# Sketched attention and a top-2 router of experts on one core: expert blocks in waves, a rebuilt attention, resident second layers

## The chip, the cores and the metric

The kernel runs on one core of a Trainium2 chip. The metric is the device time of one execution in microseconds. Every core has five engines with an instruction queue each: PE (TensorE, matrix products), DVE (VectorE), ACT (ScalarE), POOL (GpSimd) and SP (SyncE, which here only issues transfers). The engines meet by semaphores. In the profile PE's weight loads are a row of their own, PEld.

## The reference

Four batches of four heads, 1088 positions, head size 32, all in float32. Each row of q and k is projected by two 8 x 32 sketches, and the outer product of the two results gives 64 features; attention is linear in them. Its output `x` (4352 tokens of 128) goes to a router that adds scaled noise to eight logits and takes the two best of eight experts. An expert is two layers of 128 to 1024 to 128 with a relu between.

```python
phi(x) = outer(S1 x, S2 x)                       # 64 features
kv = phi(k).T @ v ;  z = phi(k).sum(seq)
x = (phi(q) @ kv) / (phi(q) @ z + 1e-6)          # heads side by side: 4352 x 128
noisy = x @ w_gate + log1p(exp(x @ w_noise)) * noise
out = sum over the top 2 experts e of  weight_e * relu(x @ w1[e]) @ w2[e]
```

## The kernel before

It has three stages, one after another.

*Attention and router*, for one batch after the other (`attention`). `key_values` transposes the keys on PE (L288), sketches them (L255), builds 64 features per head in one DVE product (L249) and sums `phk.T @ [v, 1]` over eight 128-row tiles and a rest (L304, L306). `queries` takes four tiles of queries at a time: transposes (L331), two 512-column products with both sketches (L336, L337), their product on DVE (L341), the product with `kv` (L350), and the division by the denominators (L356 to L358). `router` transposes `x` again (L369), multiplies it by the gate and noise weights (L374), runs some thirty small DVE instructions with Exp and Ln on ACT between them (L391 to L427), counts how many tokens of earlier rows go to each expert by two products with triangles and ones (L435, L436), and sends each token's two gated copies to its experts' regions of `xs` in HBM: eight indirect scatters of POOL per four tiles (L453).

*Table.* After the last token, `table` turns the counts into blocks of rows, each with an expert and a first row, read later into registers of SP (`number`, L549).

*Experts.* `blocks` walks 23 blocks of 256 rows and 21 of 128 rows mixed, then the four 256-row blocks of the fullest expert. For each, SP loads the rows (L568) and both layers of the expert, 512 KB each (L560, L561); PE transposes the rows (L596), makes the hidden layer in chunks of 512 columns (L673, here 256 columns wide for a large block), ACT or DVE applies the relu in turn (L588, L590), and the second layer follows two chunks later (L632). POOL scatters the result to `parts` (L657). Before the last expert's rows are added, `combine` sums the two parts of every token into the output; the fullest expert's rows are then added to the output by eight accumulating scatters (L648).

The order on each engine is made when the program is built, by a scheduler that takes the ready instruction of the highest priority (the earlier in the program text), with its own estimates of durations. On the chip every engine keeps to that order: PE waits at an instruction even if later ones are ready. Float32 products are shown in the trace as two records each, with a weight load each, transposes as one.

Of the kernel before, what the change touches and what calls it, by code (L numbers as in the profile page):

```python
# [8 lines left out]
F32 = mybir.dt.float32  # L9
# [12 lines left out]
def kernel(  # L22
# [14 lines left out]
    nc = tc.nc  # L37
    P = nc.NUM_PARTITIONS
# [5 lines left out]
    FJ = F // P  # L44

# [6 lines left out]
    A1 = DH + 1  # L52
# [5 lines left out]

    N = B * S
    PAIRS = 2 * N  # L60
    NL = PAIRS // E // (2 * P)
    NB = -(-(PAIRS - 2 * P * NL - E * (2 * P - 1)) // (2 * P))
    NS = (PAIRS - 2 * P * (NL + NB) + E * (P - 1)) // P
    CAP = N + P
    XW = D + 1
    I32 = mybir.dt.int32
# [4 lines left out]
    small = ctx.enter_context(tc.tile_pool(name="small", bufs=3))  # L71
    moe = ctx.enter_context(tc.tile_pool(name="moe", bufs=3))
    hpool = ctx.enter_context(tc.tile_pool(name="hpool", bufs=4))
    wpool = ctx.enter_context(tc.tile_pool(name="wpool", bufs=5))
    xpool = ctx.enter_context(tc.tile_pool(name="xpool", bufs=8))
    ypool = ctx.enter_context(tc.tile_pool(name="ypool", bufs=8))
    cpool = ctx.enter_context(tc.tile_pool(name="cpool", bufs=2))
    dram = ctx.enter_context(tc.tile_pool(name="dram", bufs=1, space=DRAM))
    ps_a = ctx.enter_context(tc.tile_pool(name="ps_a", bufs=3, space=PSUM))
    ps_h = ctx.enter_context(tc.tile_pool(name="ps_h", bufs=3, space=PSUM))  # L80
# [5 lines left out]

    words = const.tile([P, 2 * R, 2], U32, name="words")
    for i, s in enumerate((S1, S2)):
        src = s.bitcast(U32).rearrange("r (d w) -> d r w", w=2)
        for c in range(4):  # L90
            nc.scalar.dma_start(words[DH * c:DH * (c + 1), R * i:R * (i + 1), :], src)

    def u32(name):
        return const.tile([P, 2 * R], U32, name=name)

    lo_w, hi_w = words[:, :, 0], words[:, :, 1]
    expo, head, b1, b2, b3 = (u32(n) for n in ("expo", "head", "b1", "b2", "b3"))

    def bits(o, x, s1, op0, s2=None, op1=None):
        if op1 is None:  # L100
            nc.vector.tensor_scalar(out=o, in0=x, scalar1=s1, scalar2=None, op0=op0)
        else:
            nc.vector.tensor_scalar(out=o, in0=x, scalar1=s1, scalar2=s2, op0=op0, op1=op1)

    bits(expo[:], hi_w, 20, ALU.logical_shift_right, 0x7FF, ALU.bitwise_and)
    bits(expo[:], expo[:], 896, ALU.max, 896, ALU.subtract)
    bits(expo[:], expo[:], 23, ALU.logical_shift_left)
    bits(head[:], hi_w, 0x80000000, ALU.bitwise_and)
# [4 lines left out]
    for b_ in (b1, b2, b3):  # L113
        nc.vector.tensor_tensor(out=b_[:], in0=b_[:], in1=head[:], op=ALU.bitwise_or)
# [38 lines left out]
    for e in range(E):  # L153
        nc.gpsimd.memset(rank[:, e:e + 1], float(E - e))
# [599 lines left out]
```

## Time and profile before

| | |
|---|---|
| runs | 637.64, 638.33, 638.45 us (median 638.33) |
| profiled execution | 637.79 us, of which 636.1 us are the span of the trace |
| busy: PE / PEld | 469.1 us (74%) / 408.6 us (64%) |
| busy: DVE / ACT / POOL | 198.5 / 119.3 / 174.7 us |
| matrix products and transposes recorded | 2781 |
| mean granted clock of TensorE | 0.799 of full speed |
| moved by DMA | 80.27 MB, 126 GB/s |

Shares of the whole span say little here: the stages have different limits, and the rows further down give each stage apart. "Idle before" of an engine is time in which it stood before the named kind of instruction, and the releaser is what ended that wait. The ends of matrix products are modelled, so the distance between two starts says more about PE's pace than a duration.

### The profile page before, as it was taken

The numbers are of one execution on the slowest core, as the hardware profiler recorded it, in microseconds if no ns is written. First come the engines' busy times: TensorE is split into PE (matmuls) and PEld (weight loads), VectorE is DVE, ScalarE is ACT, GpSimd is POOL, SyncE is SP. The second block draws the span as 40 slices with busy tenths as digits, with TensorE's granted clock in tenths as the row PEclk, the third lists the DMA queues.
The fourth block names the chain that finished last, engine by engine and source line by source line (L and its number), as shares of the span: only waits on it lengthen the run. The fifth ranks groups of instructions, "written<-read, shape, count | busy, mean of one in ns | idle before, by whom it ended". The sixth has DMA issues, their size and how long they took to land.

```text
span 636.1 us, 8071 instructions
## 1 busy us (share of the span) xinstructions
PE 469.1 (74%) x2781; PEld 408.6 (64%) x2781; DVE 198.5 (31%) x687; ACT 119.3 (19%) x232; POOL 174.7 (27%) x236
## 2 busy tenths in 40 slices
PE   0278547847575757854518999999999999999950
PEld 0275337534563456423307999999999999999950
DVE  3112444152513451155371222222232222223430
ACT  0101330121203120132201222222212122221100
POOL 3300155106330524023420313232222313132016
PEclk9999575566557755656557999999999999999995
DMA  8841010001000100000129977868686867750753
GB/s 213 277 164 35 4 63 30 4 1 34 14 19 1 34 4 30 0 14 21 34 57 323 304 235 207 258 197 257 193 255 205 245 222 236 236 150 9 246 189 29
DMA packets 86296, 80.27 MB, mean 126 GB/s; under 512 B 11875, under 2 KB 76004, under 8 KB 85744
## 3 DMA queue, kind: packets, MB, share of 16 engines
q1 hardware_dynamic: 73152, 65.66, 33.5%
q0 software_dynamic: 5472, 8.96, 4.9%
q10 hardware_dynamic: 7632, 5.15, 2.5%
q8 instruction: 22, 0.36, 0.2%
q14 instruction: 18, 0.15, 0.1%
HBM read 63.44 MB, written 16.75 MB: 126 GB/s over the span
## 4 chain that ended last, share of the span: by engine, by line
issue 36%; PE 28%; DVE 12%; POOL 9%; DMA 6%; ACT 5%; ACTq 2%; POOLq 1%; SPq 0%; DVEq 0%
POOL parts L657 8%; PE bank L336 5%; PE bank L304 5%; PE bank L255 4%; PE bank L337 4%; DMA two<-parts 3%; PE bank L374 3%; PE bank L350 2%; PE bank L331 2%; ACT L395 2%; DVE phk L249 1%; ACT qT L334 1%; POOL out_dram L648 1%; DVE x L358 1%; DVE phq L341 1%
## 5 line engine op out<-in xcount | busy, mean ns | idle before, releaser
L673 PE MATMUL hp<-bT,w 128*128 128x256 f32 (+1 forms) x768 | 157.9, 338 | 2.4 <-DMA w<-in_moe_w_dram 2.0
L632 PE MATMUL acc<-w,h 128*128 128x128 f32 x1200 | 158.2, 275 | 0.5 <-DVE h L588 0.5
L632 PEld LDWEIGHTS acc<-w,h 128*128 128x128 f32 x1200 | 154.2, 192 | 6.2 <-DVE h L588 0.6
L673 PEld LDWEIGHTS hp<-bT,w 128*128 128x128 f32 x768 | 116.5, 194 | 9.2 <-issue 2.4
L657 POOL DMA_INDIRECT parts<-y,xb x67 | 65.8, 983 | 196.6 <-DVE y L588 147.9
L453 POOL DMA_INDIRECT xs<-xg,to x68 | 69.3, 1019 | 160.5 <-issue 59.5
L588 DVE TENSOR_SCALAR h<-hp 128x512 f32<-128x512 f32 x80 | 55.2, 691 | 120.2 <-PE hp L673 120.2
L590 ACT ACTIVATE h<-hp 128x512 f32<-128x512 f32 x70 | 41.8, 597 | 123.9 <-PE hp L673 123.9
L435 PE MATMUL bank<-masks,earlier 128*128 128x32 f32 (+1 forms) x18 | 5.4, 394 | 62.5 <-DVE g L427 62.5
L435 PEld LDWEIGHTS bank<-masks,earlier 128*128 128x128 f32 x18 | 4.5, 312 | 63.2 <-issue 63.2
L255 PE MATMUL bank<-sk,kT 128*128 128x64 f32 x136 | 29.8, 419 | 11.8 <-ACT kT L290 11.3
L304 PE MATMUL bank<-vaug,phk 128*128 128x66 f32 x128 | 29.4, 424 | 12.3 <-DVE phk L249 12.3
L255 PEld LDWEIGHTS bank<-sk,kT 128*128 128x128 f32 x136 | 29.6, 333 | 12.5 <-ACT kT L290 11.7
L336 PE MATMUL bank<-qT,sq 128*128 128x512 f32 (+1 forms) x36 | 29.9, 928 | 9.8 <-ACT qT L334 9.7
L304 PEld LDWEIGHTS bank<-vaug,phk 128*128 128x128 f32 x128 | 27.9, 330 | 13.4 <-issue 9.8
L341 DVE TENSOR_TENSOR phq<-qa,bank 128x512 f32<-128x512 f32 (+1 forms) x18 | 11.8, 658 | 59.1 <-PE bank L337 58.9
L337 PE MATMUL bank<-qT,sq 128*128 128x512 f32 (+1 forms) x36 | 27.4, 857 | 0.0
L596 PE MATMUL bank<-ident,xb 128*128 128x128 f32 x75 | 16.3, 277 | 14.0 <-DMA xb<-xs 14.0
L350 PEld LDWEIGHTS bank<-kv,phq 128*128 128x128 f32 (+1 forms) x144 | 18.2, 201 | 10.3 <-DVE phq L341 4.7
L334 ACT COPY qT<-bank 128x512 f32<-128x512 f32 (+1 forms) x18 | 10.1, 562 | 76.6 <-PE bank L331 76.6
L588 DVE COPY bT<-bank 128x256 f32<-128x256 f32 x21 | 8.9, 425 | 42.7 <-PE bank L596 42.7
L350 PE MATMUL bank<-kv,phq 128*128 128x66 f32 (+1 forms) x144 | 19.0, 285 | 3.4 <-DVE phq L341 3.4
(169 smaller groups left out, 387.5 us busy)
## 6 DMA issues: line engine op xcount, KB each, us to landing
w<-in_moe_w_dram SPq DMA_DIRECT2D x90, 512.0 KB, 4.7
parts<-zeros ACTq DMA_DIRECT2D x4, 1024.0 KB, 8.8
two<-parts SPq DMA_DIRECT2D x6, 640.0 KB, 5.6
xb<-xs SPq DMA_DIRECT2D x27, 129.0 KB, 3.7
kld<-in_k_dram SPq DMA_DIRECT2D x4, 512.0 KB, 4.9
vld<-in_v_dram SPq DMA_DIRECT2D x4, 512.0 KB, 4.0
qld<-in_q_dram SPq DMA_DIRECT2D x4, 512.0 KB, 4.4
out_dram<-one SPq DMA_DIRECT2D x6, 320.0 KB
```

What stands on the lines that cost most here:

```text
L255: nc.tensor.matmul(ps[:, c0:c0 + H * 2 * R], lhsT=kT, rhs=sk[:, i, :], start=(i == 0), stop=(i == 1))
L304: nc.tensor.matmul(o, lhsT=phk[:, t, hs, :].rearrange("p h f -> p (h f)"), rhs=vaug[:, hs, t, :], start=(t == 0), stop=False)
L336: nc.tensor.matmul(pa[:, 0:w], lhsT=sq[:, 0, :], rhs=qT[:, 0:w], start=True, stop=True)
L337: nc.tensor.matmul(pb[:, 0:w], lhsT=sq[:, 1, :], rhs=qT[:, 0:w], start=True, stop=True)
L350: nc.tensor.matmul(ps[rows, c0:c0 + 2 * A1], lhsT=phq[hp][:, P * i + rows.start:P * i + rows.stop], rhs=kv[:, hp, :], start=True, stop=True)
L374: nc.tensor.matmul(ps[:, 2 * E * i:2 * E * (i + 1)], lhsT=xT[:, P * i:P * (i + 1)], rhs=wgn[:], start=True, stop=True)
L453: disjoint("xs", nc.gpsimd.indirect_dma_start(out=xs[:], out_offset=bass.IndirectOffsetOnAxis(ap=to[:, t:t + 1], axis=0), in_=xg[:, t, :], ...
L588: nc.vector.tensor_scalar_max(o, i, 0.0) if relu else nc.vector.tensor_copy(o, i)
L590: nc.scalar.activation(out=o, in_=i, func=AF.Relu) if relu else nc.scalar.copy(o, i)
L632: nc.tensor.matmul(acc[:, D * c:D * (c + 1)], lhsT=h[:, P * (n * i + c):P * (n * i + c + 1)], rhs=w2[:, j, :], start=(j == 0 and c == 0), ...
L657: disjoint("parts", nc.gpsimd.indirect_dma_start(out=parts[:], out_offset=bass.IndirectOffsetOnAxis(ap=to[:, c, :], axis=0), in_=y[:, D * ...
L673: nc.tensor.matmul(hp[:, P * n * i:P * n * (i + 1)], lhsT=w1[:, P * (j0 + i):P * (j0 + i + 1)], rhs=xT[:, 0:P * n], start=True, stop=True)
```

## The change

All three stages are written anew; sizes, inputs, outputs and float32 stay.

- *Waves.* The tokens known after batch 0, 1 and 2 fill at least 9, 18 and 16 blocks of 128 rows whatever the routing is (`full_blocks`; 256 pairs per tile less at most 127 left over per expert). `table` now runs after every batch. Wave 0 (9 blocks) is written beside batch 2's attention, wave 1 (18) beside batch 3's, wave 2 (16) and a last wave of 32 blocks follow. All 75 blocks have 128 rows; before there were 27 of 256 and 21 of 128. A fetch waits only for the scatters of its own batch and earlier ones.
- *Second layers resident.* `load_w2` reads all eight experts' second layers (4 MB) into SBUF once. A block's transfer shrinks to its rows and `w1`. PE reads the block's expert into a register of its own (L601) and computes each of the eight operand addresses by one fused register instruction of four or five operations ("ISA" in the listings, L647).
- *Attention.* Keys and queries share `features`: transposes, a product with both halves of the sketches side by side (128 columns), an add and an outer product on DVE. Query features are then transposed for `attend`. The gate and noise weights are folded into `kv` once per batch, so that `attend` yields numerators, denominators and router scores at once (98 columns); the transposes of `x` and its product with the gate are gone.
- *Router* on 8 or 9 tiles at once instead of four (batch 0 still in two parts); its two count products use a PSUM bank of their own. ACT loads one function table at the start (L184); before, Exp and Ln changed tables 19 times.
- *Start and end.* ACT issues 3 transfers at the start instead of 37; clearing `parts` is gone. Every block scatters to `parts`; `combine` of the first 3200 tokens runs inside the last wave, and the last 1152 tokens are combined at the end in three pieces. The accumulating scatters are gone.

```diff
+    FIRST = [0, NT, 2 * NT + 1, 3 * NT + 1]
+    REST = [2 * NT, 4 * NT + 1]
+    TILES = 4 * NT + 2
+    DONE = [NT, 2 * NT + 1, 3 * NT + 1, TILES]
+    WAVES, used = [], 0
+    for d in DONE[:-1]:
+        WAVES.append(full_blocks(d) - used)
+        used += WAVES[-1]
+    LAST = (PAIRS + E * (P - 1)) // P - used
...
+    w2 = const.tile([P, E * FJ, D], F32, name="w2")
+    def load_w2():
+        for e in range(0, E, 2):
+            nc.sync.dma_start(w2[:, FJ * e:FJ * (e + 2), :],
+                              moe_w2[e:e + 2, :, :].rearrange("o (j p) d -> p (o j) d", p=P))
+    nc.scalar.preload_act_table_set("natural_log_exp_and_others")
...
+    def features(tiles, tag, by_head=False):
+        n = len(tiles)
+        ps = bank()
+        for i, x in enumerate(tiles):
+            nc.tensor.transpose(ps[:, P * i:P * (i + 1)], x, ident[:])
+        xT = work.tile([P, 512], F32, name="xT", tag="xT", bufs=3)
+        nc.scalar.copy(xT[:, 0:P * n], ps[:, 0:P * n])
+        ps = bank()
+        for i in range(n):
+            nc.tensor.matmul(ps[:, P * i:P * (i + 1)], lhsT=xT[:, P * i:P * (i + 1)],
+                             rhs=sk[:].rearrange("p i h r -> p (i h r)"), start=True, stop=True)
+        two = ps[:, 0:P * n].rearrange("p (a i b y) -> p a i b y", a=n, i=2, b=H)
+        ab = work.tile([P, G, H, 2, R], F32, name="ab", tag="ab", bufs=3)
+        o = ab[:, 0:n].rearrange("p a b w r -> p b a (w r)" if by_head else "p a b w r -> p a b (w r)")
+        nc.scalar.copy(o, two[:, :, 1])
+        V.tensor_tensor(out=o, in0=two[:, :, 0], in1=o, op=ALU.add)
+        phi = work.tile([P, G, H, RR], F32, name=tag, tag="phi", bufs=5)
+        th = ab[:, 0:n].rearrange("p t h w r -> p (t h) w r")
+        V.tensor_tensor(
+            out=phi[:, 0:n].rearrange("p t h (i j) -> p (t h) i j", i=R),
+            in0=th[:, :, 0, :].unsqueeze(3).to_broadcast([P, H * n, R, R]),
+            in1=th[:, :, 1, :].unsqueeze(2).to_broadcast([P, H * n, R, R]), op=ALU.mult)
+        return phi
...
+                    lhsT = two_heads(phis[t // G], t % G, hp)
+                    rhs = vld[:, hp, :, t, :]
+                else:
+                    lhsT = rp[r0:r0 + HALF, 2 * hp:2 * hp + 2, :].rearrange("p h f -> p (h f)")
+                    rhs = v_rest[r0:r0 + HALF, b // 2, hp, :, :]
+                nc.tensor.matmul(ps[:, W * hp:W * (hp + 1)], lhsT=lhsT, rhs=rhs, start=(t == 0 and hp == 0),
+                                 stop=(t == NT), skip_group_check=True)
+        kv = kvs[b]
+        both = ps[:, 0:2 * W].rearrange("p (a x) -> p a x", a=2)
+        upper, lower = slice(0, 2 * RR // 2), slice(RR, 2 * RR)
+        V.tensor_copy(kv[upper, :, 0:DH + 1], both[upper, :, 0:DH + 1])
...
+        ps = bank()
+        for hp in range(2):
+            nc.tensor.matmul(ps[:, 2 * E * hp:2 * E * (hp + 1)], lhsT=kvT[:, P * hp:P * (hp + 1)], rhs=wgn[:, hp, :],
+                             start=(hp == 0), stop=True, skip_group_check=True)
+        both = ps[:, 0:4 * E].rearrange("p (a x) -> p a x", a=2)
+        V.tensor_copy(kv[upper, :, KC:KC + 2 * E], both[upper, :, :])
+        nc.scalar.copy(kv[lower, :, KC + 2 * E:YC], both[lower, :, :])
...
+        phT = []
+        for hp in range(2):
+            ps = bank()
+            for i in range(n):
+                nc.tensor.transpose(ps[:, P * i:P * (i + 1)], two_heads(phi, i, hp), ident[:])
+            t = work.tile([P, 512], F32, name="phT", tag="phT", bufs=4)
+            nc.scalar.copy(t[:, 0:P * n], ps[:, 0:P * n])
...
+            ps = bank()
+            for i in range(i0, i0 + m):
+                for rows, kv in kvs_of[i]:
+                    for hp in range(2):
+                        c0 = 2 * YC * (i - i0) + YC * hp
+                        nc.tensor.matmul(
+                            ps[rows, c0:c0 + YC], lhsT=phT[hp][:, P * i + rows.start:P * i + rows.stop],
+                            rhs=kv[:, hp, :], start=True, stop=True)
+            nc.scalar.copy(nd[:, at + i0:at + i0 + m].rearrange("p t a y -> p (t a y)"), ps[:, 0:2 * YC * m])
...
-            e = number(tab, 2 * k, E - 1)
-            r = number(tab, 2 * k + 1, E * CAP)
-            return [(rows(r, n), *weights(e), n, False)]
...
+    def evict(o, i, relu=False, spread=True):
+        if spread and turn[0] % 2:
+            V.tensor_scalar_max(o, i, 0.0) if relu else V.tensor_copy(o, i)
+        else:
+            nc.scalar.activation(out=o, in_=i, func=AF.Relu) if relu else nc.scalar.copy(o, i)
+        turn[0] += 1
+    def wave(tab, step, K, spread, old=0):
...
+        def fetch(i):
+            e = value(tab, 0, i, E - 1)
+            r = value(tab, 1, i, E * CAP)
+            xb = xpool.tile([P, XW], F32, name="xb", tag="xb")
+            load_ = nc.sync.dma_start(xb[:], xs[bass.ds(r, P), :])
+            behind("xs", load_, step)
+            w1 = wpool.tile([P, F], F32, name="w1", tag="w1")
+            nc.sync.dma_start(w1[:], moe_w1[bass.ds(e, 1), :, :].rearrange("o p f -> p (o f)"))
+            fetched.append((xb, w1, i))
+        def turn_input():
+            xb, w1, i = fetched.pop(0)
+            acc = ps_o.tile([P, 512], F32, name="acc", tag="acc")
+            nc.tensor.transpose(acc[:, P:2 * P], xb[:, 0:D], ident[:])
+            xT = moe.tile([P, P], F32, name="bT", tag="bT")
+            evict(xT[:], acc[:, P:2 * P], spread=spread)
+            e = value(tab, 0, i, E - 1, PE)
+            ready.append((xb, w1, e, xT, acc))
+        def second():
+            acc, h, e, j0, xb = later.pop(0)
+            for i in range(4):
+                nc.tensor.matmul(acc[:, 0:D], lhsT=h[:, P * i:P * (i + 1)], rhs=w2[:, bass.ds(FJ * e + (j0 + i), 1), :],
+                                 start=(j0 + i == 0), stop=(j0 + i == FJ - 1))
+            if j0 + 4 < FJ:
+                return
+            y = ypool.tile([P, D], F32, name="y", tag="y")
...
+            evict(y[:], acc[:, 0:D], spread=spread)
+            disjoint("parts", nc.gpsimd.indirect_dma_start(
+                out=parts[:], out_offset=bass.IndirectOffsetOnAxis(ap=xb[:, D:XW].bitcast(U32), axis=0),
+                in_=y[:], in_offset=None, bounds_check=PAIRS - 1, oob_is_err=False), int(done[0] >= old))
+            done[0] += 1
...
+        fetch(0)
+        turn_input()
+        for b in range(K):
+            if b + 1 < K:
+                fetch(b + 1)
+            xb, w1, e, xT, acc = ready.pop(0)
+            for j0 in range(0, FJ, 4):
+                hp = ps_h.tile([P, 512], F32, name="hp", tag="hp")
+                for i in range(4):
+                    nc.tensor.matmul(hp[:, P * i:P * (i + 1)], lhsT=w1[:, P * (j0 + i):P * (j0 + i + 1)],
+                                     rhs=xT[:], start=True, stop=True)
+                h = hpool.tile([P, 512], F32, name="h", tag="h")
+                evict(h[:], hp[:], relu=True, spread=spread)
+                later.append((acc, h, e, j0, xb))
+                if len(later) > 1:
+                    second()
+                if j0 == 0 and fetched:
+                    turn_input()
+        while later:
+            second()
...
+    def attention(b, parts_):
+        kld, qld, vld = mains[b]
+        key_values(b, kld, vld)
+        tiles = [(main_features(qld, g, "phq"), [[(whole, kvs[b])]] * G) for g in range(NG)]
+        if b % 2:
...
+    for b in range(B):
+        attention(b, b == 0)
+        tabs.append(table(DONE[b], WAVES[b] if b < B - 1 else LAST, b == B - 1))
+        if b >= LEAD:
+            wave(tabs[b - LEAD], b - LEAD, WAVES[b - LEAD], b == B - 1, WAVES[b - LEAD])
+    for b in range(B - LEAD, B - 1):
+        wave(tabs[b], b, WAVES[b], True, WAVES[b])
+    ends(tabs[-1], LAST)
+    wave(tabs[-1], B - 1, LAST, True, OLD)
+    for x in combining["going"]:
...
+            pass
```

What this does to PE's queue is seen at three places. First, between the first two batches. Before, the count products (masks, before) stand directly behind the router's own products, ahead of the next queries (qx):

```order
L350 MATMUL bank<-kv_299,phq_355 128x66
L369 MATMUL bank<-ident,x 128x128 x4
L374 MATMUL bank<-wgn,xT 128x16 x4
L435 MATMUL bank<-masks,earlier 128x32
L331 MATMUL bank<-ident,qx 128x128 x4
L436 MATMUL bank<-before,ones 128x32
L336 MATMUL bank<-qT,sq 128x512
L337 MATMUL bank<-qT,sq 128x512
```

Now, with the last product of batch 0's attention (phT) on top and batch 1's keys (kld) below it:

```order
L400 MATMUL bank<-kv_167,phT 128x98 x8
L312 MATMUL bank<-ident,kld 128x128 x4
L317 MATMUL bank<-sk,xT 128x128 x4
L312 MATMUL bank<-ident,kld 128x128 x4
L317 MATMUL bank<-sk,xT 128x128 x4
L360 MATMUL bank<-vld_104,phk 128x96 x15
L473 MATMUL side<-masks,earlier 128x32
L360 MATMUL bank<-vld_104,phk 128x96
L360 MATMUL bank<-v_rest,rest_phi_306 128x96 x2
L474 MATMUL side<-before,ones 128x32
```

The count products have moved down behind 32 transposes and products of the next batch's keys and most of its key-value sums. Second, at the start of the third batch; before, it follows the second batch's router:

```order
L435 MATMUL bank<-masks,earlier 128x32
L288 MATMUL bank<-ident,kx 128x128 x7
L436 MATMUL bank<-before,ones 128x32
L288 MATMUL bank<-ident,kx 128x128
L255 MATMUL bank<-sk,kT 128x64 x16
L304 MATMUL bank<-vaug,phk 128x66 x8
L306 MATMUL bank<-vaug_rest,phk_rest 128x66
```

Now blocks of wave 0 (xb: its rows, hp: its hidden layer) stand between the steps of the keys:

```order
L312 MATMUL bank<-ident,kld 128x128 x4
L638 MATMUL acc<-ident,xb 128x128
L317 MATMUL bank<-sk,xT 128x128 x4
L312 MATMUL bank<-ident,kld 128x128 x4
L677 MATMUL hp<-bT,w_1268 128x128 x4
L317 MATMUL bank<-sk,xT 128x128 x4
L312 MATMUL bank<-ident,k_rest 128x128
L638 MATMUL acc<-ident,xb 128x128
L677 MATMUL hp<-bT,w_1268 128x128 x2
L317 MATMUL bank<-sk,xT 128x128
L360 MATMUL bank<-vld_102,phk 128x96 x8
L677 MATMUL hp<-bT,w_1268 128x128
```

About two of the nine blocks stand inside batch 2's attention, the others behind it, among its router's count products. Third, in the experts' stage. Before, with large blocks and `w_1969` a loaded first layer:

```order
L673 MATMUL hp<-bT,w_1969 128x256 x2
L632 MATMUL acc<-w_1970,h 128x128 x4
L596 MATMUL bank<-ident,xb 128x128
L673 MATMUL hp<-bT,w_1969 128x256 x2
L632 MATMUL acc<-w_1970,h 128x128 x4
L673 MATMUL hp<-bT,w_2017 128x128 x4
L632 MATMUL acc<-w_1970,h 128x128 x4
```

Now (`w_106` is the resident tensor of second layers):

```order
L677 MATMUL hp<-bT,w_2431 128x128
L638 MATMUL acc<-ident,xb 128x128
L677 MATMUL hp<-bT,w_2431 128x128 x3
L601 TENSOR_LOAD tab_953
L647 ISA
L647 MATMUL acc<-w_106,h 128x128
```

The last two rows stand four times in a row; the transposed rows of the next block go into the unused part of an `acc` bank, of which there are two.

## Rows read from the trace of the kernel before

**Rows 1.** Busy time of each engine by stretch (us), one per stage
```profile
core 0: us, PE busy (x) PEld busy (x) DVE busy (x) ACT busy (x) POOL busy (x), PEclk, DMA share, GB/s
0.00:32.00 32.00, 4.83 (x18) 3.72 (x18) 6.57 (x43) 2.10 (x3) 11.92 (x57) 1.00 0.85 246
32.00:301.00 269.00, 177.23 (x679) 133.74 (x680) 93.81 (x388) 54.90 (x96) 72.94 (x92) 0.63 0.08 28
301.00:334.60 33.60, 10.33 (x43) 7.27 (x42) 19.10 (x124) 5.24 (x11) 11.50 (x12) 0.50 0.17 46
334.60:614.20 279.60, 276.73 (x2043) 263.90 (x2043) 78.44 (x133) 57.09 (x123) 65.85 (x67) 0.99 0.72 224
614.20:636.10 21.90, 0.00 (x0) 0.00 (x0) 0.59 (x2) 0.00 (x0) 12.54 (x8) 0.61 0.30 36
```

**Rows 2.** Timeline, experts: start, length, engine, line, operation, count
```profile
410.85 1.06 PE L673 MATMUL hp<-bT,w 128*128 128x128 f32 x8
411.74 1.06 PE L632 MATMUL acc<-w,h 128*128 128x128 f32 x8
412.64 0.38 PE L596 MATMUL bank<-ident,xb 128*128 128x128 f32 x2
412.85 1.06 PE L673 MATMUL hp<-bT,w 128*128 128x128 f32 x8
...
414.64 1.03 PE L673 MATMUL hp<-bT,w 128*128 128x256 f32 x4
415.51 1.05 PE L632 MATMUL acc<-w,h 128*128 128x128 f32 x8
```

**Rows 3.** Timeline, from the start to the first key sketches
```profile
9.29 0.18 DVE L103 TENSOR_SCALAR expo<-words 128x16 uint32<-128x16 uint32 x1 [8.26 <-DMA words<-in_S_dram]
...
28.81 2.54 ACTq L243 DMA_DIRECT2D xs<-pad  x2
...
32.08 7.09 PE L255 MATMUL bank<-sk,kT 128*128 128x64 f32 x32 [11.27 <-ACT kT L290]
```

**Rows 4.** Timeline, inside the second batch, from key-values to the router
```profile
112.80 3.68 PE L304 MATMUL bank<-vaug,phk 128*128 128x66 f32 x16
...
117.03 1.11 PE L331 MATMUL bank<-ident,qx 128*128 128x128 f32 x4
...
118.24 0.59 ACT L334 COPY qT<-bank 128x512 f32<-128x512 f32 x1 [12.12 <-PE bank L331]
...
118.88 2.08 PE L336 MATMUL bank<-qT,sq 128*128 128x512 f32 x2 [0.73 <-ACT qT L334]
...
139.78 0.61 PE L435 MATMUL bank<-masks,earlier 128*128 128x32 f32 x2 [6.99 <-DVE g L427]
```

**Rows 5.** Timeline, SP's queue: two plain loads, then loads addressed by registers
```profile
0.82 0.44 SPq L171 DMA_DIRECT2D kld<-in_k_dram  x1
...
1.32 0.50 SPq L171 DMA_DIRECT2D vld<-in_v_dram  x1
...
336.45 0.39 SPq L561 DMA_DIRECT2D w<-in_moe_w_dram  x1
...
337.36 0.38 SPq L568 DMA_DIRECT2D xb<-xs  x1
...
338.24 0.34 SPq L560 DMA_DIRECT2D w<-in_moe_w_dram  x1
338.77 0.37 SPq L561 DMA_DIRECT2D w<-in_moe_w_dram  x1
```

**Rows 6.** Groups by line and shape: busy us, mean ns, idle before and releaser
```profile
L453 POOL DMA_INDIRECT xs<-xg,to x68 | 69.3, 1019 | 160.5 <-issue 59.5 <-DVE c L443 52.4 <-DVE to L446 44.0
...
L657 POOL DMA_INDIRECT parts<-y,xb x67 | 65.8, 983 | 196.6 <-DVE y L588 147.9 <-ACT y L590 32.4 <-issue 15.4
...
L590 ACT COPY y<-acc 128x128 f32<-128x128 f32 x21 | 5.6, 266 | 43.0 <-PE acc L632 43.0
...
L415 DVE TENSOR_TENSOR c<-c,rank 128x32 f32<-128x32 f32 x16 | 3.1, 192 | 0.3
```

More of the change, by code (lines that the diff above doesn't have):

```diff
@@ L458, in table @@
-    def table():
-        V = nc.vector
-        NK = NB + NS
-        ps = bank()
-        nc.tensor.matmul(ps[:, 0:E], lhsT=ones[:], rhs=before[:, TILES, :], start=True, stop=True)
-        count = small.tile([P, E], F32, name="count", tag="count", bufs=1)
-        V.tensor_copy(count[:], ps[:, 0:E])
-        def row(name, n, t=F32):
-            return small.tile([1, n], t, name=name, tag=name, bufs=1)
-        def shifted(name, src, by):
+        at = small.tile([P, 2, MOST], F32, name="at", tag="at")
@@ new lines, in table @@
+        V.tensor_tensor_scan(out=end[:, 1:S_ + 1], data0=x[:, 0:S_], data1=x[:, 0:S_], initial=0.0,
+                             op0=ALU.add, op1=ALU.bypass)
+        if not last:
+            V.tensor_scalar(out=end[:, 1:S_ + 1], in0=end[:, 1:S_ + 1], scalar1=float(K), scalar2=None, op0=ALU.min)
+            V.tensor_sub(out=x[:, 0:S_], in0=end[:, 1:S_ + 1], in1=end[:, 0:S_])
+        step = row("step", 2 * E)
+        V.tensor_sub(out=step[:, 0:S_], in0=start[:, 1:S_ + 1], in1=start[:, 0:S_])
@@ L709, with combine, piece @@
-    mains.append(load_batch(0))
-    for b in range(B):
-        attention(b)
-    qx = twice("qx", 2, lambda hp: rests["q"][:, :, 2 * hp:2 * hp + 2, :])
-    halves = [[(slice(HALF * c, HALF * (c + 1)), kvs[2 * i + c]) for c in range(2)] for i in range(2)]
-    x = queries(qx, 0, 2, halves)
-    router(x, 2, B * NT)
-    tab = table()
-    ends(tab)
-    order = []
-    for i in range(max(NB, NS)):
-        order += [(i, 2)] * (i < NB) + [(NB + i, 1)] * (i < NS)
-    order.append((None, 2))
-    blocks(tab, order)
+    def combine(t0, t1, step, C):
+        per = (t1 - t0) // P
+        src = parts[2 * t0:2 * t1, :].rearrange("(p r c) d -> p r c d", p=P, c=2)
+        dst = out[t0:t1, :].rearrange("(p r) d -> p r d", p=P)
+        def piece(r0, n):
+            two = work.tile([P, G, 2, D], F32, name="two", tag="phi", bufs=5)
+            behind("parts", nc.sync.dma_start(two[:, 0:n], src[:, r0:r0 + n]), step)
+            yield
+            V.tensor_add(out=two[:, 0:n, 0, :], in0=two[:, 0:n, 0, :], in1=two[:, 0:n, 1, :])
+            yield
+            disjoint("out", nc.sync.dma_start(dst[:, r0:r0 + n, :], two[:, 0:n, 0, :]))
+            yield
+        return [piece(r0, min(C, per - r0)) for r0 in range(0, per, C)]
```

780 lines of the change are left out of this document (336 added, 444 removed).

## The prediction, made before the changed kernel was run

> **What bounds the kernel now.** I read the busy time by stretch first, because the shares of the whole span mix stages. It shows four [rows 1]: 32 us until the first batch's keys are sketched; 269 us for four batches, 67 us each, in which PE is busy two thirds of the time at a mean granted clock of 0.63; 33.6 us of last router, table and first loads; 279.6 us of experts, in which PE is never idle for long, at 0.99; and 21.9 us at the end in which only POOL works, on eight accumulating scatters. The sum is the span of 636.1; the execution took 1.7 more, 637.8, and the median of the runs is another 0.5 higher.
>
> Then I read timelines for PE's pace. In the experts' stage eight records of 128 columns start 0.89 us apart, so 0.111 us a record; four of 256 columns take 0.87; a transpose takes 0.105 [rows 2]. [...] The attention also stands still between steps. Four transposes end PE's own work at 117.92, the copy follows, and the next product starts at 118.88: a hand-over of 0.96 us [rows 4]. The count product of the router waits 6.99 us for DVE with the next queries behind it [rows 4], twice a batch. So the first half of the kernel is bound by latency on an in-order PE, the second by PE itself. DVE and ACT are far from full.
>
> **The change part by part.** One block of 128 rows is 32 records and a transpose: 32 x 0.111 + 0.105 = 3.66 us at the upper level; 75 of them are 274 us. The work of the experts stays, and what can be gained there is only what it is placed beside. I add the new kernel up along PE's queue.
>
> *Front.* DVE starts on the sketches at 9.29, when the last of eight scattered loads has landed, and PE's first long stretch begins at 32.08 because ACT's queue still issues transfers until 31.4 [rows 3]. Now there are two loads for the sketches, then about 20 small DVE instructions (3.1 us), two transposes. I put the first key transposes at 9 us (bounds: 7, and 15 if the loads land as late as before).
>
> *Batches 0 and 1, alone.* Batch 0 has 35 transposes and 53 products, so 141 records; batch 1 with its rest of queries and the count products 161. At 0.222 that is 31 and 36 us. Hand-overs: nine and ten of 0.96 us, 9 and 9 us. The router's wait disappears from PE as long as DVE keeps up: the router of 4 tiles is about 50 instructions of 0.19 us and a dozen longer ones [rows 6], some 13 us, and the next batch's keys and key-values (some 18 us of PE) stand ahead of its count product. That gives 40 and 45 us, against 67. Whether the clock stays low is open: sums with 66 columns did not raise it [rows 4], those of the change have 96 to 128. At the upper level the records would be 33 us shorter. I take the lower level, the nearest row, and keep -33. End of batch 1: 9 + 40 + 45 = 94.
>
> *Batch 2 with wave 0.* Records now follow each other densely, so I take the upper level: attention 17 us, nine blocks 33. Some hand-overs are filled by block products, five remain (5 us). Each block adds a new wait: the next block's transpose goes to one of two `acc` banks, which is free only when the y copy is out. Drain 0.17 (1.06 less 0.89 [rows 2]), 0.10 to ACT, copy 0.27 [rows 6], 0.05 back, less the one product (0.22) that stands between: 0.35 us (0 to 0.6), so 4.0 us a block. Behind the waiting transpose stand the hidden layer and everything else on PE. DVE's router of nine tiles is late for PE's count products by some 4 us. 17 + 36 + 5 + 4 = 62.
>
> *Batch 3 with wave 1.* 18 + 18 x 4.0 + 5 + 4 = 99. The 34 scatters of batches 1 and 2 cost POOL 1.0 us each [rows 6] and lie under the waves; batch 1's 18 follow its router, which ends at about 120, and wave 1 needs them only when wave 0 ends, at 156.
>
> *Waves 2 and 3.* 48 x 4.0 = 192, and 2 us at each of two seams: 196. A block's transfers are 0.58 MB, 145 GB/s at that pace, and stay hidden: even now 224 GB/s do not stop PE [rows 1].
>
> *End.* Copy 0.5, scatter 1.0 [rows 6] and landing 2.5, load of two parts 4.5, add 0.5, store 2.4, last barrier 1.5: 13 us for 21.9.
>
> *Register addresses.* PE's queue now executes, per block, one load of the expert and eight fused register instructions. No row shows them on PE; on SP a transfer behind a fused instruction of two operations starts 0.19 us after the one before it ends (338.58 to 338.77), a plain one 0.06 us: 0.13 us. With a load as well it is 0.52, so 0.33 for the load [rows 5]. Five operations are then 0.13 to 0.33, and a block 1.4 to 3.0 us. The 66 plain instructions of a block (a weight load to each record) cost between nothing and 0.056 us each, since 16 pass in 0.89 us [rows 2]: 0 to 3.7. Together 1.4 to 6.7 us against 4.0 of the array. If it runs ahead, the queue hides it; the middle, 4.0, just does. I take nothing, with +200 us (75 x 2.7) as the upper end.
>
> [...]
>
> *Narrow blocks.* 432 records of 256 columns become 864 of 128. 0.89 against 0.87 us for the same columns [rows 2] makes that 864 x 0.0025 = 2 us, in the 3.66 already. [...]
>
> *Clock in the mixed stages.* The two mixed stages hold 134 us of records at the upper level; +134 if all of it runs at the lower. I take 10 us for their beginnings.
>
> Sum: 94 + 62 + 99 + 196 + 13 = 464, the clock 10, around the span 1.7: **476 us**, 162 less than the profiled execution. Own range 436 (batches 0 and 1 at the upper level) to 516 (first loads late, acc waits of 0.6 us, 15 us more of hand-overs).
>
> **Rivals.** *PE's sequencer is the bound* (0.18). For it: a register instruction ahead of each second-layer product, none of which is on PE today; against it: the SP rows are short and half a block's products have none. At 5.3 us a block, between the ends, 75 x 1.3 less some 12 that the hand-overs hide: about 561 us (516 to 600).
>
> *The clock stays low in the mixed stages* (0.09). For it: 0.63 in the attention with its gaps [rows 1]; against it: far fewer gaps, and 0.99 with 128-column records. About +110: 586 us.
>
> *Slower than before* (0.08). The sequencer leaves gaps in the pure waves too, and PE falls to the lower level there: a block is then 32 x 0.222 + 0.2 + 0.35 = 7.7 us, 48 of them cost 178 more, the mixed stages about 50: 704 us. It decides the sign from 6.2 us a block on (476 + 75 x 2.2 = 638). For it: the upper end of 6.7 lies above that; against: both bounds would have to be near their ends.
>
> *No overlap*: that the waves do not run beside the attention is excluded by PE's order, but they could run late if the scatters of batch 0 landed late; each us costs one, and it lies in the likeliest case's range.
>
> **How the numbers follow.** Likeliest 0.64, sequencer 0.18, clock 0.09, slower 0.08, a null 0.01. A measurement can tell about 0.2%, 1.3 us, from no change. Faster: 0.64 + 0.18 + 0.09 = 0.91; same 0.01; slower 0.08. The range 436 to 590 takes the likeliest case nearly whole, most of the sequencer's and half of the clock's: about 0.8.
>
> **What would show it.** Right: PE's first stretch at about 9 us; batch 1's last attention product near 94; blocks in waves 2 and 3 start 4.0 us apart, with a wait of some 0.35 us before the transpose put down to the y copy; granted clock near 1.0 from about 100 us on; the last second-layer product near 460. Wrong: gaps before second-layer products put down to PE's own queue (sequencer); 0.222 us a record beside waves (clock); PE waiting for `xb` at the start of a wave (scatters); waits of several us at the count products (DVE's router).

## The result, and the profile after

The changed kernel takes **450.3 us** (median of four, 447.3 to 451.5) against 638.0: ratio **0.705**, 95% interval 0.702 to 0.709, where 476 (436 to 590) was forecast. The runs below were made on four chips. On chip 7 the changed kernel takes 451 us, as here; on chip 12 it takes 511 us, and its profile has standstills that are treated below. It was not run itself on chips 4 and 1; all runs on chip 4 have such standstills, the one on chip 1 has none. The kernel before stays within 0.5% on all four. Times are compared on one chip only, or stage by stage.

The page of the changed kernel: span, busy time and granted clock.

```profile
span 447.9 us, 9408 instructions
PE 387.7 (87%) x3089; PEld 364.0 (81%) x3089; DVE 166.1 (37%) x564; ACT 113.2 (25%) x274; POOL 152.1 (34%) x207
PEclk9968867799999999998999999999999999999995
```

Busy time by stretch, as in [rows 1]: front; batch 0; batch 1; batch 2 with wave 0; batch 3 with wave 1; waves 2 and 3; end.

```profile
0.00:8.26 8.26, 0.47 (x3) 0.36 (x3) 3.55 (x30) 1.28 (x1) 6.15 (x56) 1.00 0.72 211
8.26:40.48 32.22, 27.75 (x143) 24.76 (x143) 10.09 (x24) 8.83 (x22) 0.40 (x1) 0.84 0.68 187
40.48:71.16 30.68, 24.45 (x163) 21.09 (x161) 21.65 (x121) 10.61 (x30) 13.89 (x13) 0.83 0.44 137
71.16:135.89 64.73, 55.92 (x451) 53.17 (x451) 36.48 (x162) 25.23 (x63) 31.53 (x37) 0.92 0.44 134
135.89:235.94 100.05, 91.56 (x754) 86.27 (x752) 41.10 (x120) 25.81 (x64) 51.25 (x52) 0.98 0.52 153
235.94:435.45 199.51, 187.52 (x1585) 178.39 (x1583) 51.31 (x103) 41.39 (x96) 47.91 (x48) 1.00 0.56 173
435.45:447.90 12.45, 0.00 (x0) 0.00 (x0) 1.97 (x4) 0.00 (x0) 0.98 (x1) 0.64 0.47 142
```

The saving of 188 us lies here: the front 24, the end 9, and 582 us of attention, last router and experts have become 427 in five stretches. A batch that took 67 us takes 31 to 32 where it runs alone. The clock of the first two stretches reads too high: up to 22.5 us this profile has no clock event and shows 1.00, while eight records take 1.87 us from 10.05 on, as they do at a shown clock of 0.50 (1.86 from 27.57 on). I call 0.50 the lower level and 1.00 the upper, at which eight take 0.89 (250.90 in the next listing). More on this further down.

One block in wave 2 (timeline; start, length, engine, line, idle before).

```profile
249.46 0.39 PE L677 MATMUL hp<-bT,w 128*128 128x128 f32 x2
249.71 0.29 DVE L614 COPY y<-acc 128x128 f32<-128x128 f32 x1 [2.04 <-PE acc L647]
250.06 0.14 PEld L638 LDWEIGHTS acc<-ident,xb 128*128 128x128 f32 x1 [0.41 <-DVE y L614]
250.06 0.33 PE L638 MATMUL acc<-ident,xb 128*128 128x128 f32 x1 [0.22 <-DVE y L614]
...
250.90 1.06 PE L647 MATMUL acc<-w,h 128*128 x8
...
251.79 1.06 PE L677 MATMUL hp<-bT,w 128*128 128x128 f32 x8
...
254.18 0.33 PE L638 MATMUL acc<-ident,xb 128*128 128x128 f32 x1 [0.21 <-DVE y L614]
```

Blocks start 4.12 us apart. Eight records with register addresses take 0.89 us (250.90 to 251.79), as eight of a fixed address did [rows 2]. The transpose waits for the y copy with one hidden product (two records) ahead of it: 0.41 us of the weight loads' time (PEld), 0.22 of the products'.

What ended PE's waits in the whole span (us, times, longest).

```profile
PE acc L638 <- DVE y L614: 14.7, 54, 1.7
PE acc L638 <- DMA xb<-xs: 10.2, 2, 6.7
...
PE side L473 <- DVE masks L468: 0.6, 1, 0.6
...
PE acc L647 <- issue: 0.2, 1, 0.2
```

The count products wait 0.6 us in all; before, each waited about 7 [rows 4]. PE's own queue costs the second layer 0.2 us. The two waits for rows are new. This is the longer one:

```profile
74.16 0.97 POOL L509 DMA_INDIRECT xs<-xg,to  x1 [0.30 <-issue]
...
76.66 0.37 SPq L629 DMA_DIRECT2D xb<-xs  x1
...
78.57 0.47 PE L638 MATMUL acc<-ident,xb 128*128 128x128 f32 x1 [6.75 <-DMA xb<-xs]
```

Batch 0's 16 scatters are issued 1.27 us apart from 53.3 on; the last lands at 76.5, and only then does SP fetch wave 0's first rows. Behind the waiting transpose batch 2's keys stand too.

The other is in the middle of wave 1. Below it stands what SP's queue waited for just before.

```profile
207.37 0.45 PE L638 MATMUL acc<-ident,xb 128*128 128x128 f32 x1 [3.42 <-DMA xb<-xs]
```

```profile
SPq L629 <- DMA parts<-y,xb: 13.4, 1, 13.4
```

POOL issues batch 3's 18 scatters from 180.1 to 202.7, and the blocks' own scatters to `parts` stand behind them. A block's buffer of rows is free only when its own scatter has landed; SP waits 13.4 us for that, and then PE for the rows.

### The profile page after: what moved, and what is told of

Read it like the earlier page. It is cut to its first block, busy times and chain, and to the rows that moved or that the text cites. A ratio compares the mean times of both kernels' runs of the same rounds, so it can differ in the third digit from the quotient of the medians.

```text
span 447.9 us, 9408 instructions
## 1 busy us (share of the span) xinstructions
PE 387.7 (87%) x3089; PEld 364.0 (81%) x3089; DVE 166.1 (37%) x564; ACT 113.2 (25%) x274; POOL 152.1 (34%) x207
## 4 chain that ended last, share of the span: by engine, by line
PE 63%; DMA 10%; DVE 8%; issue 8%; POOL 6%; ACT 3%; SPq 1%; DVEq 0%; ACTq 0%; POOLq 0%
PE acc L647 22%; PE hp L677 21%; PE bank L317 5%; POOL xs L509 5%; PE bank L360 4%; PE acc L638 4%; DMA two<-parts 3%; DVE y L614 3%; DMA xs<-xg,to 3%; PE bank L400 3%; DMA xb<-xs 2%; PE bank L312 2%; DMA parts<-y,xb 1%; PE bank L389 1%; POOL parts L653 1%
## 5 line engine op out<-in xcount | busy, mean ns | idle before, releaser
L677 PE MATMUL hp<-bT,w 128*128 128x128 f32 x1200 | 172.8, 278 | 1.2 <-ACT bT L616 1.1
L647 PE MATMUL acc<-w,h 128*128 x1200 | 160.9, 277 | 0.3 <-issue 0.2
L677 PEld LDWEIGHTS hp<-bT,w 128*128 128x128 f32 x1200 | 156.6, 196 | 2.5 <-ACT bT L616 1.7
L647 PEld LDWEIGHTS acc<-w,h 128*128 128x128 f32 x1200 | 147.3, 193 | 1.2 <-issue 1.0
L653 POOL DMA_INDIRECT parts<-y,xb x75 | 75.8, 1010 | 199.2 <-DMA xb<-xs 115.8
L614 DVE COPY y<-acc 128x128 f32<-128x128 f32 x66 | 19.1, 290 | 121.7 <-PE acc L647 111.4
L638 PE MATMUL acc<-ident,xb 128*128 128x128 f32 x75 | 24.2, 325 | 26.4 <-DVE y L614 14.7
L616 ACT COPY bT<-acc 128x128 f32<-128x128 f32 x75 | 19.9, 266 | 83.6 <-PE acc L638 83.6
L317 PE MATMUL bank<-sk,xT 128*128 128x128 f32 x136 | 27.8, 360 | 7.1 <-ACT xT L314 7.1
L317 PEld LDWEIGHTS bank<-sk,xT 128*128 128x128 f32 x136 | 23.4, 256 | 11.1 <-ACT xT L314 11.0
L400 PE MATMUL bank<-kv,phT 128*128 128x98 f32 (+1 forms) x144 | 18.7, 283 | 1.3 <-ACT phT L391 1.2
L360 PE MATMUL bank<-vld,phk 128*128 128x96 f32 x128 | 18.4, 306 | 0.3 <-DVE phk L326 0.3
```

The costliest lines, as they stand in the source:

```text
L317: nc.tensor.matmul(ps[:, P * i:P * (i + 1)], lhsT=xT[:, P * i:P * (i + 1)], rhs=sk[:].rearrange("p i h r -> p (i h r)"), start=True, stop= ...
L360: nc.tensor.matmul(ps[:, W * hp:W * (hp + 1)], lhsT=lhsT, rhs=rhs, start=(t == 0 and hp == 0), stop=(t == NT), skip_group_check=True)
L400: nc.tensor.matmul(ps[rows, c0:c0 + YC], lhsT=phT[hp][:, P * i + rows.start:P * i + rows.stop], rhs=kv[:, hp, :], start=True, stop=True)
L614: V.tensor_scalar_max(o, i, 0.0) if relu else V.tensor_copy(o, i)
L616: nc.scalar.activation(out=o, in_=i, func=AF.Relu) if relu else nc.scalar.copy(o, i)
L638: nc.tensor.transpose(acc[:, P:2 * P], xb[:, 0:D], ident[:])
```

## The experiments

**All waves behind all attention** (chip 4).

```diff
-            behind("xs", load_, step)
+            behind("xs", load_, B - 1)
-    LEAD = 2
+    LEAD = B
```

> All waves stand behind all four batches' attention, and no block is fetched before the last scatter; everything else is the changed kernel's. Theory: the overlap itself is worth little, because the changed kernel's attention alone takes 31 to 32 us a batch. Sum from its trace: 8.3 until the first key transpose, 32 for batch 0, 3 x 31, some 20 to 25 for the last router, table, scatters and first rows, 75 blocks x 4.12, 12.5 at the end, 1.7 around: 476 to 482 us, 27 to 32 above 450. Rival: putting the waves beside the attention is the main gain, and without it the attention goes back to 45 to 67 us a batch: 530 to 600 us.

515.7 us, ratio 0.805 (0.800 to 0.811). PE's wait ahead of the first block:

```profile
206.90 0.47 PE L638 MATMUL acc<-ident,xb 128*128 128x128 f32 x1 [28.23 <-DMA xb<-xs]
```

The attention ends at 160, and the last router, table and 18 scatters keep PE idle until 206.9, 47 us for the 20 to 25 of the sum. This run has standstills in the attention too (batch 1 takes 40 us). My sum was too small (the 18 scatters alone take 23 of the 47 us), the rival's 530 to 600 too large: with the waves last, and with standstills, the kernel is still 123 us faster than before. Without standstills I estimate 8 + 4 x 31 + 47 + 75 x 3.90 + 14 = 486, so the overlap would be worth some 35 us. Its blocks are 3.90 us apart, though, for 4.12 in the changed kernel (the next experiment says why); with equal blocks it would be some 52. Neither was run.

**A fixed address for the second layer** (chip 4).

```diff
-            e = value(tab, 0, i, E - 1, PE)
+            e = 0
-    ... rhs=w2[:, bass.ds(FJ * e + (j0 + i), 1), :],
+    ... rhs=w2[:, j0 + i, :],
```

> Every block takes expert 0's second layer at a fixed address (the choice of the second layer is left out), so PE's queue has no register load and no register arithmetic; its products and transfers are as many and as long. Theory: PE's sequencer runs ahead of the array and the addresses are hidden: 450 us within 2. Rival: the register instructions leave gaps in the stages where PE waits for others, or pace the blocks: 435 to 446 us, with blocks under 4.05 us apart in the pure waves.

483.9 us; without a control on chip 4 the total says little. Blocks of the pure waves are 3.68 us apart:

```profile
401.11 0.27 PE L638 MATMUL acc<-ident,xb 128*128 128x128 f32 x1
...
404.12 0.83 PE L677 MATMUL hp<-bT,w 128*128 128x128 f32 x6
404.37 0.29 DVE L614 COPY y<-acc 128x128 f32<-128x128 f32 x1 [2.04 <-PE acc L647]
404.79 0.27 PE L638 MATMUL acc<-ident,xb 128*128 128x128 f32 x1
404.79 0.30 PEld L677 LDWEIGHTS hp<-bT,w 128*128 128x128 f32 x2
...
405.01 0.97 PEld L647 LDWEIGHTS acc<-w,h 128*128 128x128 f32 x8
```

That is the rival's number, and its reason holds for half of it. Without the register instructions the scheduler has put the transpose behind three hidden products (six records) instead of one, and the y copy is out in time. The serial kernel, with registers, has that order as well. The wait for `y` is gone there too, but its blocks are 3.90 us apart:

```profile
401.34 0.27 PE L638 MATMUL acc<-ident,xb 128*128 128x128 f32 x1
...
405.24 0.27 PE L638 MATMUL acc<-ident,xb 128*128 128x128 f32 x1
405.24 0.30 PEld L677 LDWEIGHTS hp<-bT,w 128*128 128x128 f32 x2
...
405.68 0.97 PEld L647 LDWEIGHTS acc<-w,h 128*128 128x128 f32 x8
```

From the weight loads of the hidden product to those of the second layer 0.44 us pass, for 0.22 at the fixed address. The block's register load and its first arithmetic stand there, and behind the transpose one product covers them, where the changed kernel has three. So the order alone is worth 0.22 of the 0.44 us of a block, and the other 0.22 go with the register instructions. In the changed kernel's own order they cost nothing that shows: the own-bank run below has them, and blocks 3.68 us apart.

**A register load ahead of every product of the second layer** (chip 4).

```diff
             for i in range(4):
+                x_ = value(tab, 0, e, E - 1, PE)
-    ... bass.ds(FJ * e + (j0 + i), 1) ...
+    ... bass.ds(FJ * x_ + (j0 + i), 1) ...
```

> PE loads the expert's number from SBUF anew ahead of each of a block's eight products of the second layer, so eight loads and eight pieces of arithmetic a block for one and eight. It asks how far the sequencer is from being the bound. By the durations on SP (0.33 a load, 0.13 a pair of operations) a block costs the sequencer 3.7 us and what its 66 plain instructions cost, 0 to 3.7. Theory (plain instructions are nearly free to the sequencer, so the kernel has a margin of about 2.5 us a block): 450 to 475 us. Rival (the plain instructions take near their upper end and the changed kernel is just under the edge): 7 us a block, so about 650 us.

618.1 us, ratio 0.962 (0.952 to 0.971); blocks 5.6 us apart, at a mean granted clock of 0.98 (430 to 590 us). The weight loads (the queue's own time shows as "issue"):

```profile
503.60 0.30 PEld L647 LDWEIGHTS acc<-w,h 128*128 128x128 f32 x2 [0.24 <-issue]
504.14 0.30 PEld L647 LDWEIGHTS acc<-w,h 128*128 128x128 f32 x2 [0.24 <-issue]
```

A load, its arithmetic and one product take 0.54 us of the queue. The trace has the first two on PE's own queue (ns, shortest, median, longest):

```profile
L601 PEldq TENSOR_LOAD <-tab x600: 294/298/798, 89.0 to 603.6; - x150
...
L647 PEldq FUSED_REGOPS  x600: 60/64/69, 89.6 to 604.0; - x150
```

SP's prices, 0.33 and 0.13 [rows 5], leave an estimated 0.08 for the four plain instructions, 0.02 each. The changed kernel's block is then 0.33 + 8 x 0.13 + 66 x 0.02 = 2.7 us by estimate (2.1 with PE's own 0.30 and 0.064 and the same 0.02), under its 3.68 of the array. The margin is real but not wide: my theory's 450 to 475 fell, and seven more loads made the queue the bound.

**A bank of its own for the transpose, in waves 2 and 3** (chip 4).

```diff
-            nc.tensor.transpose(acc[:, P:2 * P], xb[:, 0:D], ident[:])
+            tp, c0 = (bank(), 0) if step >= B - LEAD else (acc, P)
+            nc.tensor.transpose(tp[:, c0:c0 + P], xb[:, 0:D], ident[:])
```

> In waves 2 and 3 the transpose of a block's rows goes to one of the three banks that the attention no longer uses, instead of the accumulation bank of the block before the last. Theory: the wait of about 0.39 us ahead of each of those 47 transposes, for the y copy, goes, and nothing is late behind it: 450 - 47 x 0.39 = about 432 us, blocks 3.7 us apart. Rival: the first product of the second layer needs the same bank 1.9 us later and the copies of x or h become the wait: at most 5 us less, 445 to 450.

491.3 us. The total says nothing without its control, the stage does: waves 2 and 3 take 180.3 us from the first transpose to the start of the last products, against 199.0 in the control on chip 12: 18.7 less, blocks 3.68 apart:

```profile
399.91 0.27 PE L639 MATMUL bank<-ident,xb 128*128 128x128 f32 x1
...
403.59 0.27 PE L639 MATMUL bank<-ident,xb 128*128 128x128 f32 x1
```

The theory holds.

**The control, and the bank in all waves** (chip 12).

> The changed kernel itself once more, as the control of the other runs. In the first four experiments ACT, DVE and PE stood still for stretches of 3 to 16 us beside the scatters of batches 1 to 3, for which the trace names no cause; the first trace of the changed kernel has none of them. If they belong to the place where those runs were made, this run takes 485 to 510 us with the same stretches; if the edits made them, 450 us without.

511.5 us (506 to 514), ratio 0.796 (0.792 to 0.800), so the edits did not make the standstills; the same kernel has them on this chip and not on chip 7. One of them:

```profile
115.31 0.48 PE L638 MATMUL acc<-ident,xb 128*128 128x128 f32 x1 [5.26 <-ACT y L616]
...
115.58 1.06 PE L677 MATMUL hp<-bT,w 128*128 128x128 f32 x4
...
116.43 1.91 PE L647 MATMUL acc<-w,h 128*128 x8
117.62 0.97 POOL L509 DMA_INDIRECT xs<-xg,to  x1 [0.30 <-issue]
...
121.33 0.27 ACT L616 COPY bT<-acc 128x128 f32<-128x128 f32 x1 [6.08 <-remote]
...
121.65 2.08 PE L677 MATMUL hp<-bT,w 128*128 128x128 f32 x8 [3.31 <-issue]
```

PE's transpose is over at 115.8 and PE goes on with 12 further records, but ACT copies its result only at 121.33 and the profile names no releaser. The long waits of this kind that I followed are of ACT, DVE or SP for PE, beside POOL's back-to-back scatters (1.27 us apart); what waits for DVE or ACT goes on at once (PE 0.05 us after the copy at 121.33).

```diff
+            tp = bank()
-            nc.tensor.transpose(acc[:, P:2 * P], xb[:, 0:D], ident[:])
+            nc.tensor.transpose(tp[:, 0:P], xb[:, 0:D], ident[:])
```

> As the experiment with a bank of its own for the transpose of a block's rows, but in all four waves; in waves 0 and 1 the three banks are shared with the attention's steps. Theory: in the pure waves blocks are 3.68 us apart, as in that trace, for 4.12; in the mixed stages 27 more waits of 0.39 us go, 10 us, if the attention's own steps do not wait for their banks in turn: 28 us less than the control in all. Rival: the banks are short in the mixed stages and the gain there turns into a loss: 10 to 20 us less than the control.

499.2 us, 12 less than the control: the rival's range. In the profiled executions, which are 8 us apart, waves 2 and 3 gain 18 and 10 are lost before: wave 0's first transpose now comes at 109.5 us for 82.8, since in PE's order it stands behind all of batch 2's attention.

**Narrower key-value sums** (chip 12, one execution).

```diff
-                nc.tensor.matmul(ps[:, W * hp:W * (hp + 1)], lhsT=lhsT, rhs=rhs, ...
+                w_ = W if t in (0, NT) else 2 * DH
+                r_ = rhs if w_ == W else vld[:, hp, 0:2, t, :]
+                nc.tensor.matmul(ps[:, W * hp:W * hp + w_], lhsT=lhsT, rhs=r_, ...
```

> The products of keys and values of a batch's eight tiles but the first have 64 columns for 96 (the second head's numerators of those tiles are left out); nothing else changes. PE works 112 x 32 columns less, 1.5 us in all. Theory: the granted clock rose to the upper level in the middle of these products in batch 0 because of their width; with 64 columns batches 0 and 1 stay at the lower level and take about 40 and 45 us, so the kernel is 15 to 23 us slower than the control. Rival: the clock follows the missing waits, not the width: batches 0 and 1 as in the control, total within 3 us of it.

520.7 us. Batch 0 takes 34.1 us for 32.1, batch 1 43.4 for 42.0. The sums themselves:

```profile
17.14 6.93 PE L362 MATMUL bank<-vld,phk 128*128 128x96 f32 x32
```

6.93 us for 6.22 with 96 columns. In the control the clock rises at 22.2 us, near the end of these sums, and in the eleven other profiles with sums of this width at 12.9 to 23.0; here it first rises at 38.3. The direction is the theory's, the size 2 to 4 us, not 15 to 23. That the width is the reason isn't shown: this is one execution, and in the last run below the clock rises at 12.9, before the sums begin at 15.8. The rest of the 9 us stays open among standstills.

**Both layers streamed, nothing resident** (chip 12).

```diff
+            w2b = wpool.tile([P, FJ, D], F32, name="w2b", tag="w2b")
+            nc.sync.dma_start(w2b[:], moe_w2[bass.ds(e, 1), :, :] ...)
...
-            e = value(tab, 0, i, E - 1, PE)
-            ready.append((xb, w1, e, xT, acc))
+            ready.append((xb, w1[0], w1[1], xT, acc))
...
-    ... rhs=w2[:, bass.ds(FJ * e + (j0 + i), 1), :],
+    ... rhs=e[:, j0 + i, :],
```

> Both layers of a block's expert are fetched for each block, 1.09 MB for 0.58 a block, nothing is kept resident and PE has no register address; the arithmetic is the same. At the control's pace a block needs 265 GB/s; slices of the trace of the change show up to 319. Theory: PE still sets the pace and residency is worth little: within 10 us of the control, slower only where scatters and batches' loads share the queues. Rival: transfers set the pace at the 224 GB/s that the stage of experts of before had: 4.9 us a block, about 50 us slower than the control.

493.3 us, ratio 0.768 (0.765 to 0.771), 18 less than the control. The stretch from 290 to 480, and the same length of the control:

```profile
290.00:480.00 190.00, 182.51 (x1525) 176.17 (x1525) 49.55 (x101) 39.40 (x91) 45.93 (x46) 1.00 0.98 307
```

```profile
300.00:490.00 190.00, 177.33 (x1503) 168.99 (x1503) 49.02 (x98) 38.81 (x90) 44.69 (x45) 1.00 0.59 178
```

307 GB/s and the transfer engines 98% busy. Both guesses were wrong on the sign, but the edit changes two things: with the resident layers PE's register instructions go too (`e` is now the fetched tile). The kernel with a fixed address has neither the registers nor the transfers of second layers, and beside it streaming costs time. Up to wave 2's first transpose the two are alike, at 287.7 and 287.5 us (297.4 in the control, 298.0 in the own-bank run on chip 4), so the 10 us gained there are not streaming's. Waves 2 and 3, from that transpose to the last product's start, then take 197.6 us for 182.4 at the fixed address and 200.7 in the control. The first blocks are 3.68 us apart, most later ones 4.01 or more in another order of the scheduler's, and PE waits for first layers (285 to 490 us), which the fixed-address kernel does not:

```profile
PE hp L673 <- DMA w<-in_moe_w_dram: 5.6, 5, 1.4
```

So residency is worth up to 15 us in these waves; the profiled execution of the streamed kernel, 499.7 us, lies 6 above its median, and how much of the 15 that takes isn't known.

**Scatters spread over the waves, and then the bank** (chip 7).

```diff
-                disjoint("xs", nc.gpsimd.indirect_dma_start(... to[:, i, t:t + 1] ...), step)
+                if step:
+                    held.setdefault(step, []).append((scatter, t, i))
+                else:
+                    scatter(t, i)
...
+            for _ in range(RATE.get(step, (0, 0))[done[0] % 2]):
+                if held.get(step + 1):
+                    f, t, i_ = held[step + 1].pop(0)
```

> The changed kernel once more, as the control of the two runs beside it. If it is run where PE's signals are held back beside bursts of scatters, about 511 us; if not, about 450.

450.7 us: chip 7 has no standstills.

> The scatters of rows of batches 1, 2 and 3 no longer go out in a burst of 16 or 18 behind their router, but behind the scatters of blocks, 3, 1 and 1 to 2 to a block of the wave that needs them last (waves 0, 1 and 2); nothing else changes. In the traces with stretches of standstill ACT, DVE and SP wait only for PE, though PE's work is long done and it goes on with other products, and the stretches end with POOL's bursts. Theory: PE's signals are held back while POOL issues transfers back to back, so without bursts the stretches go: where the control takes 511 us, 450 to 480; where the control takes 450, within 5 us of it. Rival: the stretches come with the number of scatters or with the place of the waves: 505 to 515 where the control takes 511.

449.1, ratio 0.701 (0.697 to 0.705) against the control's 0.704 (0.700 to 0.709): no change, as expected for such a chip. Whether it ends standstills elsewhere was not seen.

> As the run before it, and in waves 2 and 3 the transpose of a block's rows has a bank of its own. Theory: the two gains add up, since the second lies in the pure waves, 45 blocks x 0.44 us = 20 us: about 20 us less than the run before it, so 430 to 460. Rival: with scatters of batch 3 in wave 2 the blocks of that wave are no longer 3.68 us apart and half of the 20 us is gone.

434.0, ratio 0.680 (0.676 to 0.684), 3.7% under the control, and 15 us under the run before it, where 20 were expected. Batch 0 and the last waves:

```profile
8.47:36.67 28.20, 23.49 (x143) 20.70 (x143) 10.10 (x24) 8.73 (x22) 0.40 (x1) 1.00 0.63 173
...
231.80:418.10 186.30, 180.02 (x1584) 178.98 (x1584) 50.97 (x103) 41.40 (x96) 64.70 (x66) 0.99 0.68 201
```

Waves 2 and 3 take 186.3 us for 199.8 in the control, at 3.68 us a block, so the rival did not come. Another 4 us are batch 0's: the clock rose at 21.6 and stayed up, where it fell back at about 26 in the control. Nothing in the edit explains that.

> The version with spread scatters and a bank of its own in waves 2 and 3 once more, to see it in another place. Theory: 434 us where PE's signals are not held back; where they are (control 511 us, the version with the bank alone 491), 440 to 460, because there are no bursts beside the waves any more and only batch 0's 16 scatters are left in one. Rival: as late as with bursts, 480 to 495 there.

431.0, ratio 0.675 (0.673 to 0.678), on chip 1, without standstills: the version is confirmed. The changed kernel was not run there, so a chip that has none can't be told from one where spreading the scatters ended them.

## Why the prediction was right

The mechanism held: PE's in-order queue, added up stage by stage. Term by term, forecast and measured in us:

| term | forecast | measured |
|---|---|---|
| front | 9 | 8.3 |
| batch 0 | 40 | 32.2 |
| batch 1 | 45 | 30.7 |
| batch 2 with wave 0 | 62 | 64.7 |
| batch 3 with wave 1 | 99 | 100.1 |
| waves 2 and 3 | 196 | 199.5 |
| end | 13 | 12.4 |
| clock in the mixed stages | 10 | in the stages |
| around the span | 1.7 | 1.7 |

**Batches 0 and 1** are the mis-sized term, 22 us of the 26, and the step that was off is the lower level taken for every record. The same eight records of the key sketches, at 10.05 and, in batch 1, at 41.81, up to what follows them:

```profile
10.05 2.08 PE L317 MATMUL bank<-sk,xT 128*128 128x128 f32 x8 [0.68 <-ACT xT L314]
11.92 1.06 PE L312 MATMUL bank<-ident,kld 128*128 128x128 f32 x4
...
41.81 1.16 PE L317 MATMUL bank<-sk,xT 128*128 128x128 f32 x8 [0.73 <-ACT xT L314]
42.80 0.60 PE L312 MATMUL bank<-ident,kld 128*128 128x128 f32 x4
```

They take 1.87 and 0.99 us, the lower and the upper level (at 41.81 the granted clock is 1.00). The clock was up from 22.5 to 25.9 us, from 36.1 to 53.2 and from 63.4 on, so for a quarter of batch 0 and two thirds of batch 1. From start to start, as I took the 0.222 (7.09 us for 32 records, [rows 3]) and the 0.96, I estimate 26 us of records in batch 0 for my 31 and 23 in batch 1 for my 36: 18 of the 22 us. The hand-overs, 8 and 11 of 0.4 to 1.4 us, come to about 6 and 8 us for my 9 each; the plain ones are as long as before, 0.9 us, shown as 0.68 to 0.73 of idle time. Why the clock rose is open. My lower bound, the upper level throughout, was nearer than my choice (33 us off 476 give 443, though; the 436 stated has 7 more that no term names).

**Mixed stages**: right in sum, with errors that cancel. DVE's router is not late (0.6 us for my 4 in each). Instead PE waits 6.75 us at the start of wave 0, one of my signs of being wrong, for the late scatters that I had set aside as a few us of the likeliest range. It waits another 3.42 us in wave 1, where scatters did not simply lie under the waves: POOL's burst held up the blocks' own. A scatter takes 1.27 us of POOL's time in a burst, not 1.0. The lower level up to 83.9 us and for 3.4 us at 206.8 cost some 4 of the 10 us for the clock, by estimate from the records in them.

**Block**: the acc wait of 0.35 came as 0.41, 4.12 us for 4.0; over 48 blocks that is 5.8 us, and the seams took some 2 less than their 4. The own-bank runs show its cause and its price.

**Sequencer**: hidden, as chosen, and the rival at 561 did not come. Its run shows where it would have: at 0.54 us for each product with a load of its own. That nothing was lost is in part luck of the order: in the serial kernel's order the same instructions cost 0.22 us a block. In the changed kernel the second layer's products wait 0.2 us for PE's own queue in the whole span; with a load before each product the gaps of 0.24 us show that the queue did not hide a steady stream of them.

**Narrow blocks**: eight records of 128 columns take 0.89 us in this trace as before, and blocks whose transpose has a bank of its own are 3.68 us apart, where I had 3.66 for their records and a transpose.

**Clock and slower cases**: from 84 us until PE is done the granted clock is at the upper level but for 3.4 us. With standstills, on chip 12, the mixed stages fall to the lower level while PE waits (eight records shown as 2.08 us at 121.65, for 1.06 at the upper), and the same kernel takes 511 us, still inside the range.

## What to carry to other kernels

Add up the queue of the engine that bounds, stage by stage, with durations of the same shapes; errors then stay in single terms. Where a buffer is handed from a late reader to an early writer, look at how many instructions of the bound engine stand between: here, with one product between, the transpose waited and a block took 0.44 us longer; with three it did not wait, and a spare bank gave 2.4% and 3.4% of the kernel in two runs. Before crediting an overlap or a resident operand, run the kernel without it, and change nothing else: streaming both layers looked faster, but the register addresses had gone with the resident ones.

## What the runs showed of the hardware that was not expected

- On chip 12 and in the runs on chip 4, instructions of ACT, DVE and SP started up to 16 us (in the control) after the PE work that they need was over, while POOL issued scatters 1.27 us apart; what needed ACT or DVE went on at once. On chip 12 the changed kernel lost 61 us by it and the kernel before at most 0.5%. Why, and why not on chip 7, stays open, as does whether spreading the scatters cures it.
- A register load, its arithmetic and a product cost PE's queue 0.54 us, the load itself 0.30 and the arithmetic 0.064. One load and eight pieces of arithmetic a block cost nothing that shows with three products behind the load, and 0.22 us with one.
- Transfers ran at 307 GB/s for 190 us with the 16 engines 98% busy, beside a PE that was busy 96% of that time.
